# v as two adjacent keys per partition: a chunked attention in front of two feed-forward layers, on one Trainium2 core

## The chip, the cores and the metric

The program runs on 1 core of one Trainium2 chip. The metric is the device time of one execution in microseconds (us). The engines are named as the profile names them: PE (TensorE), PEld (its weight loads), DVE (VectorE), ACT (ScalarE), POOL (GpSimd) and SP (SyncE, which here only issues DMAs).

## What is computed

```python
q_c = q.reshape(B, H, nc, 64, D)              # B = H = 8, 576 tokens = 9 chunks of 64, D = 64; k_c, v_c alike
scores = (1 / np.sqrt(D)) * np.matmul(q_c, k_c.transpose(0, 1, 2, 4, 3))
scores = scores - np.max(scores, axis=-1, keepdims=True)
attn = np.exp(scores)
attn = attn / (np.sum(attn, axis=-1, keepdims=True) + 1e-09)
out = np.matmul(attn, v_c)
x = out.transpose(0, 2, 1, 3).reshape(4608, 512)
# logits = x @ w_gate; each of 8 experts takes 576 tokens, the largest logits first
# expert e: x = relu(x @ w1[e]) @ w2[e]
# last layer: max(x @ m1, x @ m2, x @ m3) @ m_out
```

## The kernel before, in words

The attention works on 9 units of 512 tokens (8 chunks of 64), each unit in 4 groups of 128 tokens with all 8 heads, 36 groups in all. The loop at L245 runs over the groups, and in iteration i it does one step of each of several groups: the scores of group i (`scores`, L124), the transposes and evacuations of a quarter of the q and k of the next unit (`trans`, `evac`, L105 and L117), the transposes of the weights of group i-1 (`att_t`, L164) and their product with v (`pv`, L175), and the scaling, storing and transposing of the result of group i-2 (`scale`, `x_t`, L185 and L192). The order of the calls is the order on each engine's queue. Once in four iterations a unit's logits are computed in two steps: `logit1` (L206, a product with w_gate in four column tiles) and `logit2` (L223, transposes and a sum on DVE), both through the PSUM bank pL.

v lies in three rotating buffers VB (L89). A buffer's partition is 64·s + key for head 2·hp + s, and its free part is [chunk, hp, s', d] with zeros where s' differs from s. So `pv` multiplies a stationary 128x64 tile (the transposed weights of two heads of one chunk) with 128 columns, 8 times in a group, in two column tiles of PE. A load of v (`load_v`, L65) writes 64 partitions; its contiguous pieces are one key of one head, 256 bytes. The zeros are written once at the start, half of them by two instructions for each buffer (L91, L92).

The loads of a unit's v are issued one unit ahead and those of q and k two units ahead, on SP's queue (half of v's on POOL's). At the top of each iteration SP issues a small DMA of the last maximum (`tick`, L249). It waits for that maximum, so that the loads behind it on SP's queue keep pace with the groups.

PSUM has 8 banks: pT has two buffers, pS takes two banks, and pA, pX, pY and pL have one each.

After the attention a router assigns the tokens in rounds, one for each expert (`Router.round`, L502). When the first round has named its expert, three 512 KB pieces ("chunks") of that expert's weights are issued on SP (L962 to L964), then POOL gathers the expert's 576 tokens in five indirect DMAs (`gather`, L793), and a second `tick` (L973) holds SP until the last of the five has landed. Each chunk is split into a high part by ACT (`split_hi`, L756) and a low part by DVE (`split_lo`, L765). A planner places these: `issue` (L744) gives a chunk a due time, 10 slots after its issue (16 for every eighth), `pump` (L946) moves the clock on by one slot per half of a product of 12 matmuls and calls `bulk` (L778), which splits a chunk whose time has come; `have` (L1017) splits at once what the next product needs. From the second expert on, PE has work throughout.

Of the kernel before, what the change touches and what calls it, by code (L numbers as in the profile page):

```python
# [7 lines left out]
F32 = mybir.dt.float32  # L8
# [20 lines left out]
def attention(ctx, tc, q, k, v, wg_in, xd, L, ident, consts, early, tick, mark):  # L29

    nc = tc.nc
    C = ctx.enter_context(tc.tile_pool(name="ac", bufs=1))
    P = ctx.enter_context(tc.tile_pool(name="aw", bufs=2))
    PS = ctx.enter_context(tc.tile_pool(name="aps", bufs=2, space=PSUM))
    QK, QT, KBT, PT, PSS, MX, A, R, PA, AT, PX, X, PY, XT, LS = ({} for _ in range(15))

    ORDER = [0, 1, 2, 3, None, 4, 5, 6, 7]

    def chunk(u, j):

        b = ORDER[u]
        return (b, b % 2 + j) if b is not None else (j, 0 if j % 2 else 8)
# [21 lines left out]

    def load_v(u, part):  # L65

        t = VB[u % 3]
        if ORDER[u] is not None:
            b, c = chunk(u, 0)
            for s in range(2):  # L70
                (nc.gpsimd if u and s else nc.sync).dma_start(
                    t[s * 64:(s + 1) * 64, :, part, s, :],
                    bass.AP(tensor=v.tensor, offset=v.offset + (b * H + 2 * part + s) * S * D + c * 64 * D,
                            ap=[[D, 64], [64 * D, 8], [1, D]]))
            return
        for j in (2 * part, 2 * part + 1):
            b, c = chunk(u, j)
            for s in range(2):
                (nc.gpsimd if u and s else nc.sync).dma_start(
                    t[s * 64:(s + 1) * 64, j, :, s, :],  # L80
                    bass.AP(tensor=v.tensor, offset=v.offset + b * H * S * D + s * S * D + c * 64 * D,
                            ap=[[D, 64], [2 * S * D, 4], [1, D]]))
# [6 lines left out]
    VB = [C.tile([128, 8, 4, 2, 64], F32, name="vb%d" % i) for i in range(3)]  # L89
    for t, eng in ((VB[0], nc.vector), (VB[1], nc.gpsimd), (VB[2], nc.gpsimd)):  # L90
        eng.memset(t[0:64, :, :, 1, :], 0.0)  # L91
        eng.memset(t[64:128, :, :, 0, :], 0.0)  # L92
    nc.scalar.dma_start(wg[:, :, :8], wg_in.rearrange("(a p) e -> p a e", p=128))
    consts()
    warm = PS.tile([128, 4, 128], F32, name="pA", bufs=1)
# [9 lines left out]
    def trans(nm, u, n, bank="pT"):  # L105

        mark(nm + "T")
        if n == 0:
            QT[nm, u] = P.tile([128, 4, 8, 64], F32, name=nm + "T")
        pt = PS.tile([128, 2, 2, 128], F32, name=bank, bufs=2 if bank == "pT" else 1)  # L110
        PT[nm, u, n] = pt
        for a in range(2):
            for w in range(2):
                h = 4 * (n // 2) + 2 * a + n % 2
                nc.tensor.transpose(pt[:, a, w, :], QK[nm, u][:, h, w * 128:w * 128 + 128], ident)  # L115

    def evac(nm, u, n, r, eng):  # L117
        mark(nm + "E")
        s, h0 = n % 2, 2 * (n // 2)
        src = PT[nm, u, n][r * 64:r * 64 + 64].rearrange("p a w t -> p a t w")  # L120
        dst = QT[nm, u][s * 64:s * 64 + 64, h0:h0 + 2].rearrange("p a j (i w r) -> p a (j i) w r", w=2, r=2)[:, :, :, :, r]
        (nc.vector.tensor_copy if eng else nc.scalar.copy)(dst, src)

    def scores(g):  # L124
        mark("scores")
        u, h = divmod(g, 4)
        PSS[g] = PS.tile([128, 2, 512], F32, name="pS", bufs=1)[:, :, :256].rearrange("p s (a i) -> p a s i", a=4)
        for hp in range(4):
            for c in range(2):
                for s in range(2):  # L130
                    o, to = slice(s * 64, s * 64 + 64), slice(c * 64, c * 64 + 64)
                    nc.tensor.matmul(PSS[g][to, hp, s], QT["q", u][o, hp, 2 * h + c], QT["k", u][o, hp, 2 * h + c],  # L132
                                     start=True, stop=True, tile_position=(s * 64, c * 64))
# [11 lines left out]

    def expo(g):
        mark("exp")
        e = P.tile([128, 8, 64], F32, name="A")
        nc.scalar.activation(e, A[g], AF.Exp, scale=0.125)
        A[g] = e  # L150

    def sums(g, st):
        mark("sums")
        if st == 0:
            R[g] = P.tile([128, 8], F32, name="sm")
            nc.vector.tensor_reduce(R[g], A[g], op=OP.add, axis=AX.X)
        elif st == 1:
            nc.vector.tensor_scalar(R[g], R[g], 1e-9, None, op0=OP.add)
        else:
            r = P.tile([128, 8], F32, name="rc")  # L160
            nc.vector.reciprocal(r, R[g])
            R[g] = r

    def att_t(g):  # L164
        mark("attT")
        PA[g] = PS.tile([128, 4, 128], F32, name="pA", bufs=1)
        for hp in range(4):
            nc.tensor.transpose(PA[g][:, hp, :], A[g][:, 2 * hp:2 * hp + 2, :], ident)  # L168

    def att_c(g):  # L170
        mark("attTc")
# [3 lines left out]
    def pv(g):  # L175
        mark("pv")
        u, h = divmod(g, 4)
        PX[g] = PS.tile([128, 4, 128], F32, name="pX", bufs=1)
        for hp in range(4):
            for c in range(2):  # L180
                nc.tensor.matmul(PX[g][c * 64:(c + 1) * 64, hp, :], AT[g][:, hp, c * 64:c * 64 + 64],  # L181
                                 VB[u % 3][:, 2 * h + c, hp].rearrange("p s i -> p (s i)"),
                                 start=True, stop=True)

    def scale(g):  # L185
        mark("scale")
        X[g] = P.tile([128, 8, 64], F32, name="x", bufs=3)
        nc.vector.tensor_tensor(X[g], PX[g].rearrange("p a (s i) -> p (a s) i", s=2),
                                R[g][:, :, None].to_broadcast([128, 8, 64]), op=OP.mult)
# [16 lines left out]
    def logit1(j, w0=0, w1=4):  # L206
        mark("logit1")
        t = slice(w0 * 128, w1 * 128)
        pl = PS.tile([128, 512], F32, name="pL", bufs=1)
        for dc in range(4):  # L210
            nc.tensor.matmul(pl[32 * dc:32 * dc + 32, t], wg[:, dc, :], XT[j][:, dc, t],
                             start=True, stop=True, tile_position=(0, 32 * dc))
        LS[j] = P.tile([128, 512], F32, name="ls")
        nc.scalar.copy(LS[j][:, t], pl[:, t])

    def logit(j, w):
        mark("logit")
        pl = PS.tile([128, 4, 128], F32, name="pT")
        for dc in range(4):
            nc.tensor.matmul(pl[:, 0, :E], XT[j][:, dc, w * 128:(w + 1) * 128], wg[:, dc, :E], start=dc == 0, stop=dc == 3)  # L220
        nc.vector.tensor_copy(L[:, columns(j)[w], :], pl[:, 0, :E])

    def logit2(j, w0=0, w1=4):  # L223
        mark("logit2")
        pl = PS.tile([128, 4, 4, 32], F32, name="pL", bufs=1)
        for w in range(w0, w1):
            nc.tensor.transpose(pl[:, w].rearrange("p a e -> p (a e)"), LS[j][:, w * 128:(w + 1) * 128], ident)
        to = columns(j)
        step = to[1] - to[0]
        nc.vector.tensor_reduce(L[:, to[w0]:to[w1 - 1] + 1:step, :],  # L230
                                pl[:, w0:w1, :, :8].rearrange("p w a e -> p w e a"), op=OP.add, axis=AX.X)

    banks = iter(("pT", "pT", "pX", "pY", "pL", "pA", "pT", "pT"))
    for n in (0, 2):
        for nm in "kq":
            for i in (n, n + 1):
# [4 lines left out]
    def on(j):  # L241
        return 0 <= j < G

    LOADS = [[("k", 0), ("q", 0)], [("k", 4)], [("q", 4)], []]
    for i in range(G):  # L245
        u, n = i // 4 + 1, i % 4
# [11 lines left out]
            scale(i - 2)  # L258
        if on(i):
            smax(i)  # L260
        if on(i - 1):
            att_t(i - 1)
            att_c(i - 1)
            if i < G - 1:
                sums(i - 1, 0)
# [17 lines left out]
        if on(i - 1):  # L283
            pv(i - 1)
            sums(i - 1, 1)
            sums(i - 1, 2)
        if i >= 7 and (i - 4) % 4 == 3 and i < G - 1:
            logit2((i - 4) // 4)
        if i >= 6 and (i - 3) % 4 == 3 and i < G:
            logit1((i - 3) // 4)  # L290
        if on(i - 2):
            x_c(i - 2)

# [16 lines left out]
    early(2)  # L310
    for st in (1, 2, 3):
        early(0, st)
    logit(8, 2)
    logit2(8, 0, 2)
    logit(8, 3)


class Clock:
# [381 lines left out]
def kernel(ctx, tc, q, k, v, w_gate, w1, w2, m1, m2, m3, m_out, out, mark=lambda n: None):  # L700
# [259 lines left out]
    rt.begin(PS)  # L960
    first = rt.round(0, PS, expert)
    while next(first) is not None:  # L962
        if state["issued"] < 3:
            issue()  # L964
    xg = gather(0)
    rt.warm(PS, 24)
# [3 lines left out]
            pass  # L970
        rt.warm(PS, (6, 5)[i])

    nc.sync.dma_start(tick[:, 4:5], xg[4][0:1, 0:1])  # L973

    split()
    XO, WA, WB, Y = {}, [], [], []
# [318 lines left out]
```

## Time and profile before

| | us |
|---|---|
| median of 3 runs (lowest to highest) | 1206.3 (1203.97 to 1208.42) |
| the profiled execution's own time | 1207.02 |
| its span, from the first to the last instruction | 1205.2 |
| PE busy | 1172.5 (97%) |
| DVE busy | 830.5 (69%) |
| ACT busy | 412.7 (34%) |
| POOL busy | 317.9 (26%) |

The shares are means over stages that differ: the attention takes about the first 165 us, the first round of the router the next 25, and the experts and the last layer the rest. How the rows are read: a row of the timeline has its start, its length, engine, line, operation, tiles, and in brackets how long the engine was idle before it and what ended that. A tile's name stands for all its buffers. An fp32 matmul shows as two instructions, a transpose as one.

### The profile page before, as it was taken

To read this page: it belongs to the slowest core of one execution; us is meant where nothing else is said; L and a number is where in the kernel's file an instruction comes from. 1 tells how busy PE (TensorE), PEld (TensorE's weight loads), DVE (VectorE), ACT (ScalarE), POOL (GpSimd) and SP (SyncE) were. 2 spreads that over 40 slices of the span, in tenths; PEclk is the share of its full clock that TensorE was granted. 3 is DMA by queue.
4 is the path that set the end of the run, shared out by engine and by line. 5 is a ranking of instruction groups with operands and counts; after the bars stand their busy time and mean duration, and the time that the engine had idled before them with its cause. 6 is when DMAs were issued, how large, how long until landed. Compare 5 with 4: busy or idle time off the path is not lost.

```text
span 1205.2 us, 23575 instructions
## 1 busy us (share of the span) xinstructions
PE 1172.5 (97%) x9508; PEld 1097.6 (91%) x9508; DVE 830.5 (69%) x1660; ACT 412.7 (34%) x674; POOL 317.9 (26%) x507
## 2 busy tenths in 40 slices
PE   7999978999999999999999999999999999999998
PEld 6788856989999999989999998998998998998996
DVE  6888976788898888888843565565565565664661
ACT  5888823232333333325423113113113113113111
POOL 8433201010337463766770002002002002002002
PEclk9999989999999999999999999999999999999999
DMA  9999516264566565559834773773773763773651
GB/s 264 256 271 269 162 45 184 66 233 150 177 193 209 184 215 183 186 192 283 281 144 162 274 259 123 276 260 119 280 259 118 281 259 115 285 258 114 235 189 53
DMA packets 138828, 242.99 MB, mean 202 GB/s; under 512 B 30048, under 2 KB 101216, under 8 KB 131808
## 3 DMA queue, kind: packets, MB, share of 16 engines
q1 hardware_dynamic: 118608, 180.90, 45.9%
q0 software_dynamic: 14976, 51.13, 12.7%
q10 hardware_dynamic: 5136, 9.46, 2.1%
q8 instruction: 75, 1.23, 0.4%
q14 instruction: 33, 0.27, 0.1%
HBM read 195.05 MB, written 46.40 MB: 200 GB/s over the span
## 4 chain that ended last, share of the span: by engine, by line
PE 53%; issue 35%; DMA 4%; DVE 3%; POOL 2%; ACT 1%; POOLq 1%; SPq 1%; ACTq 0%; DVEq 0%
PE acc L1105 17%; PE acc L1050 16%; DMA vb<-in_v_dram 3%; PE pX L181 2%; PE py L1143 2%; POOL out_dram L1227 2%; PE pT L115 2%; PE po L1219 2%; PE px L1143 2%; PE pz L1143 2%; PE pS L132 1%; PE pA L168 1%; PE pxt L821 1%; PE pY L199 1%; PE rp L553 1%
## 5 line engine op out<-in xcount | busy, mean ns | idle before, releaser
L1050 PE MATMUL acc<-xhi,chunk 128*128 128x288 f32 (+2 forms) x1024 | 207.4, 302 | 2.7 <-DVE hlo L1083 2.3
L1105 PE MATMUL acc<-hhi,chunk 128*128 128x288 f32 x1024 | 209.9, 299 | 0.0
L1227 POOL DMA_INDIRECT out_dram<-ot,ia x36 | 36.3, 1008 | 519.4 <-ACT ot L1225 518.8
L1050 PEld LDWEIGHTS acc<-xhi,chunk 128*128 128x128 f32 x1024 | 161.9, 189 | 3.8 <-DVE hlo L1083 2.7
L1105 PEld LDWEIGHTS acc<-hhi,chunk 128*128 128x128 f32 x1024 | 163.0, 188 | 0.3
L1105 PE MATMUL acc<-hlo,chunk 128*128 128x288 f32 x512 | 150.9, 295 | 0.0
L1219 PE MATMUL po<-chunk,h 128*128 128x512 f32 x648 | 149.3, 390 | 0.0
L1219 PEld LDWEIGHTS po<-chunk,h 128*128 128x128 f32 x648 | 121.5, 188 | 24.8
L1050 PE MATMUL acc<-xlo,chunk 128*128 128x288 f32 (+2 forms) x512 | 143.9, 296 | 0.0
L1143 PE MATMUL px<-xb,wa 128*128 128x384 f32 x648 | 130.0, 335 | 0.7 <-ACT ys L1112 0.7
L1143 PE MATMUL py<-xt,wb 128*128 128x384 f32 x648 | 129.9, 335 | 0.0
L1143 PEld LDWEIGHTS px<-xb,wa 128*128 128x128 f32 x648 | 113.9, 188 | 1.4 <-ACT ys L1112 1.0
L1143 PEld LDWEIGHTS py<-xt,wb 128*128 128x128 f32 x648 | 114.0, 188 | 0.5
L1164 ACT CAST h<-best 128x384 fp32r<-128x384 f32 x72 | 37.0, 513 | 198.1 <-DVE best L1162 121.3
L1105 PEld LDWEIGHTS acc<-hlo,chunk 128*128 128x128 f32 x512 | 96.2, 188 | 0.0
L1050 PEld LDWEIGHTS acc<-xlo,chunk 128*128 128x128 f32 x512 | 94.1, 189 | 0.0
L768 DVE TENSOR_TENSOR chunk<-raw,chunk 128x1024 fp32r<-128x1024 f32 x67 | 84.8, 1271 | 6.5 <-ACT chunk L761 5.7
L1074 ACT ACTIVATE hhi<-acc 128x576 fp32r<-128x576 f32 (+1 forms) x66 | 41.8, 637 | 137.2 <-PE acc L1050 135.3
L798 POOL DMA_INDIRECT xg<-xd,idx x40 | 43.3, 1082 | 169.2 <-DVE ohe L688 89.7
L1179 ACT COPY tmp<-px 128x384 f32<-128x384 f32 x54 | 25.8, 478 | 146.3 <-PE px L1143 146.3
L761 ACT CAST chunk<-raw 128x1024 fp32r<-128x1024 f32 x67 | 69.7, 1047 | 7.8 <-ACT ys L1112 6.4
L1083 DVE SCALAR_TENSOR_TENSOR hlo<-acc,hhi 128x576 fp32r<-128x576 f32 (+1 forms) x66 | 48.2, 735 | 30.9 <-ACT hhi L1074 30.5
(222 smaller groups left out, 2058.5 us busy)
## 6 DMA issues: line engine op xcount, KB each, us to landing
wb<-wdb SPq DMA_DIRECT2D x54, 1024.0 KB
wa<-wda SPq DMA_DIRECT2D x54, 768.0 KB
raw<-in_moe_w_dram SPq DMA_DIRECT2D x64, 512.0 KB
xd<-x POOLq DMA_DIRECT2D x36, 256.0 KB, 4.8
yd<-ys ACTq DMA_DIRECT2D x32, 288.0 KB
wdb<-pair POOLq DMA_DIRECT2D x18, 512.0 KB, 4.7
yraw<-yd SPq DMA_DIRECT2D x12, 768.0 KB
ink<-in_k_dram SPq DMA_DIRECT2D x16, 512.0 KB
```

The lines of the kernel that those rows point to most:

```text
L761: nc.scalar.copy(hi, raw)
L768: nc.vector.tensor_tensor(lo, raw, hi.bitcast(F32), op=OP.subtract)
L798: nc.gpsimd.indirect_dma_start(out=g, out_offset=None, in_=xd[:, :], in_offset=bass.IndirectOffsetOnAxis(ap=rt.idx[r][:, t:t + 1], axis=0))
L1050: nc.tensor.matmul(acc[:, hf, :tk.stop - tk.start], w[a][:, dc, o:o + 128], x[:, dc, tk], start=n == 0, stop=n == 11)
L1074: nc.scalar.activation(hv, src, AF.Relu)
L1083: nc.vector.scalar_tensor_tensor(lv, src, 0.0, hv.bitcast(F32), op0=OP.max, op1=OP.subtract)
L1105: nc.tensor.matmul(acc[:, hf, :288], w[a][:, f, :], x[:, f, tk], start=n == 0, stop=n == 23)
L1143: nc.tensor.matmul(dst, w[:, dc, o, a], XO[x][:, c, dc], start=start and n == 0, stop=stop and n == 5, skip_group_check=True)
L1164: nc.scalar.copy(hpart(g, i, j)[0], M)
L1179: nc.scalar.copy(U[g, 1], XB[g])
L1219: nc.tensor.matmul(PO[t], h[:, x, t % 6 * 128:t % 6 * 128 + 128], w[a][:, f % 2], start=f == 0 and n == 0, stop=f == 5 and n == 2)
L1227: st = nc.gpsimd.indirect_dma_start(out=out, out_offset=bass.IndirectOffsetOnAxis(ap=ia[:, t:t + 1], axis=0), in_=ot, in_offset=None)
```

## The change

v is laid out anew: a partition holds two adjacent keys of a head, so that a contiguous piece is 512 bytes, and a load writes 32 partitions. A buffer's partition is 64·i + 32·s + key pair, its free part [chunk, x, s', r, d], and the head is 4·i + 2·s + x. Each buffer is cleared by one instruction. The keys of k are left in the order in which the transposes give them (contiguous evacuations), and `scores` reads them in the order (r, i, w), two neighbouring columns lying 512 bytes apart. The exponential writes its result in the order that the new product wants, and the sums are taken over two axes. `pv` becomes 16 products of 64x64 tiles in place of 8 of 128x64, in two accumulating steps, and its result takes two PSUM banks. In exchange pL is given up: the logits use the two buffers of pT, and stand at another place of the loop, between the scores and the transposes of the weights, `logit1` one iteration later than before. Ahead of the first gather SP issues two chunks of weights and not three, and the `tick` behind the gather waits for its third piece and not for the fifth.

```diff
     def load_v(u, part):
-        t = VB[u % 3]
...
+        t, (x, i) = VB[u % 3], divmod(part, 2)
+        for s in range(2):
+            rows, head = slice(64 * i + 32 * s, 64 * i + 32 * s + 32), 4 * i + 2 * s + x
+            for e in range(1 if ORDER[u] is not None else 2):
+                b, c = chunk(u, e)
+                dst, n, step = (t[rows, :, x, s], 8, 64 * D) if ORDER[u] is not None else (t[rows, e::2, x, s], 4, 2 * H * S * D)
                 (nc.gpsimd if u and s else nc.sync).dma_start(
...
+                    dst.rearrange("p j r d -> p j (r d)"),
+                    bass.AP(tensor=v.tensor, offset=v.offset + (b * H + head) * S * D + c * 64 * D,
+                            ap=[[2 * D, 32], [step, n], [1, 2 * D]]))
...
-        eng.memset(t[0:64, :, :, 1, :], 0.0)
-        eng.memset(t[64:128, :, :, 0, :], 0.0)
+        eng.memset(t, 0.0)
...
     def evac(nm, u, n, r, eng):
...
+        if nm == "k":
+            src = PT[nm, u, n][r * 64:r * 64 + 64]
+            dst = QT[nm, u][s * 64:s * 64 + 64, h0:h0 + 2].rearrange("p a j (x t) -> p a (j x t)", x=2).rearrange(
+                "p a (r w t) -> p a r w t", r=2, w=2)[:, :, r]
...
     def scores(g):
...
+        keys = QT["k", u].rearrange("p a j x -> p a (j x)").rearrange("p a (r w j i) -> p a j r i w", r=2, w=2, j=8)
...
-                    nc.tensor.matmul(PSS[g][to, hp, s], QT["q", u][o, hp, 2 * h + c], QT["k", u][o, hp, 2 * h + c],
+                    nc.tensor.matmul(PSS[g][to, hp, s], QT["q", u][o, hp, 2 * h + c], keys[o, hp, 2 * h + c],
                                      start=True, stop=True, tile_position=(s * 64, c * 64))
...
     def expo(g):
-        e = P.tile([128, 8, 64], F32, name="A")
-        nc.scalar.activation(e, A[g], AF.Exp, scale=0.125)
+        e = P.tile([128, 4, 4, 32], F32, name="A")
+        nc.scalar.activation(e.rearrange("t n a p -> t a n p"), A[g].rearrange("t (a s) (r p) -> t a (s r) p", s=2, r=2),
+                             AF.Exp, scale=0.125)
...
-            nc.vector.tensor_reduce(R[g], A[g], op=OP.add, axis=AX.X)
+            nc.vector.tensor_reduce(R[g].rearrange("t (a s) -> t a s", s=2), A[g].rearrange("t (s r) a p -> t a s r p", r=2),
+                                    op=OP.add, axis=AX.XY)
...
     def pv(g):
...
-        PX[g] = PS.tile([128, 4, 128], F32, name="pX", bufs=1)
-        for hp in range(4):
-            for c in range(2):
-                nc.tensor.matmul(PX[g][c * 64:(c + 1) * 64, hp, :], AT[g][:, hp, c * 64:c * 64 + 64],
-                                 VB[u % 3][:, 2 * h + c, hp].rearrange("p s i -> p (s i)"),
-                                 start=True, stop=True)
+        PX[g] = PS.tile([128, 2, 512], F32, name="pX", bufs=1)
+        for x in range(2):
+            for r in range(2):
+                for c in range(2):
+                    for i in range(2):
+                        o = slice(i * 64, i * 64 + 64)
+                        nc.tensor.matmul(PX[g][c * 64:(c + 1) * 64, i, :256].rearrange("p (s x d) -> p x s d", s=2, x=2)[:, x],
+                                         AT[g][o, 2 * x + r, c * 64:c * 64 + 64], VB[u % 3][o, 2 * h + c, x, :, r],
+                                         start=r == 0, stop=r == 1, tile_position=(i * 64, c * 64))
...
     def logit1(j, w0=0, w1=4):
-        pl = PS.tile([128, 512], F32, name="pL", bufs=1)
+        pl = PS.tile([128, 512], F32, name="pT")
...
     def logit2(j, w0=0, w1=4):
-        pl = PS.tile([128, 4, 4, 32], F32, name="pL", bufs=1)
+        pl = PS.tile([128, 4, 4, 32], F32, name="pT")
...
         if on(i):
             smax(i)
+        if i >= 7 and i % 4 == 3:
+            logit1(i // 4 - 1)
+        if i >= 8 and i % 4 == 0:
+            logit2(i // 4 - 2)
         if on(i - 1):
             att_t(i - 1)
...
-        if i >= 7 and (i - 4) % 4 == 3 and i < G - 1:
-            logit2((i - 4) // 4)
-        if i >= 6 and (i - 3) % 4 == 3 and i < G:
-            logit1((i - 3) // 4)
...
-        if state["issued"] < 3:
+        if state["issued"] < 2:
             issue()
...
-    nc.sync.dma_start(tick[:, 4:5], xg[4][0:1, 0:1])
+    nc.sync.dma_start(tick[:, 4:5], xg[2][0:1, 0:1])
```

Left out: the scaling reads the two banks of the product, the first unit's transposes go to pX's two halves and not to pL, and the last token's logits use the bank pY.

## Rows read from the trace of the kernel before

**Rows 1.** The page: DMA busy share in 40 slices of 30 us.
```profile
DMA  9999516264566565559834773773773763773651
```

**Rows 2.** Stretches (us): length, busy PE, PEld, DVE, ACT, POOL, PE clock, DMA share, GB/s.
```profile
20.00:30.00 10.00, 8.84 (x134) 7.63 (x132) 6.58 (x12) 5.69 (x10) 7.66 (x24) 0.83 1.14 279
...
40.00:60.00 20.00, 18.22 (x275) 15.32 (x274) 15.44 (x31) 15.30 (x28) 10.13 (x18) 0.91 1.10 252
...
64.87:80.73 15.86, 15.86 (x270) 13.23 (x272) 14.30 (x30) 14.32 (x26) 6.58 (x11) 1.00 1.10 271
```

**Rows 3.** Timeline of PE, 16.9 to 58 us: the waits for loads.
```profile
19.66 0.44 PE L181 MATMUL pX<-vb,AT 128*64 128x128 f32 x4 [1.78 <-DMA vb<-in_v_dram]
...
22.47 1.09 PE L115 MATMUL pT<-ident,inq 128*128 128x128 f32 x4 [1.16 <-DMA inq<-in_q_dram]
...
55.74 0.44 PE L181 MATMUL pX<-vb,AT 128*64 128x128 f32 x4 [1.78 <-DMA vb<-in_v_dram]
```

**Rows 4.** The chain of waits: start, length, what.
```profile
41.70 13.90 DMA vb<-in_v_dram
```

**Rows 5.** Timeline of PE, 101 to 106 us: one iteration without logits.
```profile
101.75 0.69 PE L132 MATMUL pS<-kT,qT 64*64 64x64 f32 x32
102.38 0.66 PE L168 MATMUL pA<-ident,A 128*128 128x128 f32 x4
...
104.28 1.09 PE L181 MATMUL pX<-vb,AT 128*64 128x128 f32 x16
105.30 0.69 PE L132 MATMUL pS<-kT,qT 64*64 64x64 f32 x32
```

**Rows 6.** Timeline of DVE, 102 to 107 us: one iteration without logits.
```profile
102.34 0.69 DVE L188 TENSOR_TENSOR x<-pX,rc 128x512 f32<-128x512 f32 x1
102.95 0.68 DVE L138 TENSOR_REDUCE mx<-pS 128x8 f32<-128x512 f32 x1
...
104.91 0.69 DVE L122 COPY kT<-pT 64x512 f32<-64x512 f32 x1
...
106.14 0.69 DVE L188 TENSOR_TENSOR x<-pX,rc 128x512 f32<-128x512 f32 x1
```

**Rows 7.** Groups by form, 0 to 175 us: busy us, mean ns, idle before.
```profile
L230 DVE TENSOR_REDUCE L<-pL 128x32 f32<-128x128 f32 x8 | 2.3, 290 | 0.2
```

**Rows 8.** DMA totals of three stretches: 4 to 11, 13 to 17, 206 to 207.4 us.
```profile
DMA packets 2885, 2.39 MB, mean 341 GB/s; under 512 B 568, under 2 KB 2885, under 8 KB 2885
...
DMA packets 3041, 0.78 MB, mean 195 GB/s; under 512 B 3029, under 2 KB 3040, under 8 KB 3040
...
DMA packets 846, 0.43 MB, mean 308 GB/s; under 512 B 5, under 2 KB 846, under 8 KB 846
```

**Rows 9.** Waits of PEld, 64.5 to 144 us: total, times, longest.
```profile
PEld pS L132 <- issue: 6.5, 17, 0.8
...
PEld pX L181 <- issue: 1.7, 10, 0.2
```

**Rows 10.** Timeline by engine, 184 to 262 us: first gather, splitting of weights, one wait.
```profile
188.48 1.06 POOL L798 DMA_INDIRECT xg<-xd,idx  x1 [21.96 <-DVE idx L682]
...
193.56 0.66 PE L821 MATMUL pxt<-ident,xg 128*128 128x128 f32 x4 [1.58 <-DMA xg<-xd,idx]
...
202.98 1.22 DVE L768 TENSOR_TENSOR chunk<-raw,chunk 128x1024 fp32r<-128x1024 f32 x1
...
211.32 0.32 PEld L1050 LDWEIGHTS acc<-xhi,chunk 128*128 128x128 f32 x2
...
211.75 1.22 DVE L768 TENSOR_TENSOR chunk<-raw,chunk 128x1024 fp32r<-128x1024 f32 x1
...
214.92 0.24 PE L566 MATMUL rp<-cs,lev 128*128 128x8 f16 x4 [0.61 <-DVE cs L558]
```

**Rows 11.** The tile xg: time from issue to landing of its 40 DMAs.
```profile
DMA to landing us min/median/max: 3.4/4.2/7.3
```

**Rows 12.** Weight loads by form, 185 to 189 us (72 bytes between columns).
```profile
L665 PEld LDWEIGHTS <-aoh 128*32 128x32 bf16 x36 | 0.6, 155 | 0.7 <-DVE aoh L642 0.7
```

More of the change, by code (lines that the diff above doesn't have):

```diff
@@ L65, in load_v @@
     def load_v(u, part):
-        t = VB[u % 3]
-        if ORDER[u] is not None:
-            b, c = chunk(u, 0)
-            for s in range(2):
-                (nc.gpsimd if u and s else nc.sync).dma_start(
[L72 to L82, printed above, removed]
+        t, (x, i) = VB[u % 3], divmod(part, 2)
[4 more added lines that the diff above has]
+                dst, n, step = (t[rows, :, x, s], 8, 64 * D) if ORDER[u] is not None else (t[rows, e::2, x, s], 4, 2 * H * S * D)
+                (nc.gpsimd if u and s else nc.sync).dma_start(
+                    dst.rearrange("p j r d -> p j (r d)"),
+                    bass.AP(tensor=v.tensor, offset=v.offset + (b * H + head) * S * D + c * 64 * D,
+                            ap=[[2 * D, 32], [step, n], [1, 2 * D]]))
     for h in (0, 4):
@@ L88, in attention @@
     nc.vector.memset(wg, 0.0)
-    VB = [C.tile([128, 8, 4, 2, 64], F32, name="vb%d" % i) for i in range(3)]
+    VB = [C.tile([128, 8, 2, 2, 2, 64], F32, name="vb%d" % i) for i in range(3)]
     for t, eng in ((VB[0], nc.vector), (VB[1], nc.gpsimd), (VB[2], nc.gpsimd)):
-        eng.memset(t[0:64, :, :, 1, :], 0.0)
-        eng.memset(t[64:128, :, :, 0, :], 0.0)
+        eng.memset(t, 0.0)
     nc.scalar.dma_start(wg[:, :, :8], wg_in.rearrange("(a p) e -> p a e", p=128))
@@ L109, in trans @@
             QT[nm, u] = P.tile([128, 4, 8, 64], F32, name=nm + "T")
-        pt = PS.tile([128, 2, 2, 128], F32, name=bank, bufs=2 if bank == "pT" else 1)
+        if isinstance(bank, str):
+            pt = PS.tile([128, 2, 2, 128], F32, name=bank, bufs=2 if bank == "pT" else 1)
+        else:
+            pt = bank.rearrange("p (a w t) -> p a w t", a=2, w=2)
         PT[nm, u, n] = pt
@@ L120, in evac @@
         src = PT[nm, u, n][r * 64:r * 64 + 64].rearrange("p a w t -> p a t w")
-        dst = QT[nm, u][s * 64:s * 64 + 64, h0:h0 + 2].rearrange("p a j (i w r) -> p a (j i) w r", w=2, r=2)[:, :, :, :, r]
+        if nm == "k":
+            src = PT[nm, u, n][r * 64:r * 64 + 64]
+            dst = QT[nm, u][s * 64:s * 64 + 64, h0:h0 + 2].rearrange("p a j (x t) -> p a (j x t)", x=2).rearrange(
+                "p a (r w t) -> p a r w t", r=2, w=2)[:, :, r]
+        else:
+            dst = QT[nm, u][s * 64:s * 64 + 64, h0:h0 + 2].rearrange("p a j (i w r) -> p a (j i) w r", w=2, r=2)[:, :, :, :, r]
         (nc.vector.tensor_copy if eng else nc.scalar.copy)(dst, src)
@@ L166, in att_t @@
         PA[g] = PS.tile([128, 4, 128], F32, name="pA", bufs=1)
-        for hp in range(4):
-            nc.tensor.transpose(PA[g][:, hp, :], A[g][:, 2 * hp:2 * hp + 2, :], ident)
+        for n in range(4):
+            nc.tensor.transpose(PA[g][:, n, :], A[g].rearrange("t n a p -> t n (a p)")[:, n], ident)
     def att_c(g):
@@ L177, in pv @@
         u, h = divmod(g, 4)
-        PX[g] = PS.tile([128, 4, 128], F32, name="pX", bufs=1)
-        for hp in range(4):
-            for c in range(2):
-                nc.tensor.matmul(PX[g][c * 64:(c + 1) * 64, hp, :], AT[g][:, hp, c * 64:c * 64 + 64],
-                                 VB[u % 3][:, 2 * h + c, hp].rearrange("p s i -> p (s i)"),
-                                 start=True, stop=True)
+        PX[g] = PS.tile([128, 2, 512], F32, name="pX", bufs=1)
[7 more added lines that the diff above has]
+                                         start=r == 0, stop=r == 1, tile_position=(i * 64, c * 64))
     def scale(g):
@@ L187, in scale @@
         X[g] = P.tile([128, 8, 64], F32, name="x", bufs=3)
-        nc.vector.tensor_tensor(X[g], PX[g].rearrange("p a (s i) -> p (a s) i", s=2),
-                                R[g][:, :, None].to_broadcast([128, 8, 64]), op=OP.mult)
+        nc.vector.tensor_tensor(X[g].rearrange("p (i h) d -> p i h d", i=2),
+                                PX[g][:, :, :256].rearrange("p i (h d) -> p i h d", d=64),
+                                R[g].rearrange("p (i h) -> p i h", i=2)[:, :, :, None].to_broadcast([128, 2, 4, 64]), op=OP.mult)
         nc.gpsimd.dma_start(xd[tokens(g) * 128:(tokens(g) + 1) * 128, :], X[g].rearrange("p h d -> p (h d)"))
@@ L214, in logit1, with logit @@
         nc.scalar.copy(LS[j][:, t], pl[:, t])
-    def logit(j, w):
+    def logit(j, w, bank):
         mark("logit")
-        pl = PS.tile([128, 4, 128], F32, name="pT")
+        pl = PS.tile([128, 4, 128], F32, name=bank, bufs=2 if bank == "pT" else 1)
         for dc in range(4):
@@ L231, in logit2 @@
                                 pl[:, w0:w1, :, :8].rearrange("p w a e -> p w e a"), op=OP.add, axis=AX.X)
-    banks = iter(("pT", "pT", "pX", "pY", "pL", "pA", "pT", "pT"))
+    px = PS.tile([128, 2, 512], F32, name="pX", bufs=1)
+    banks = iter(("pT", "pT", "pY", px[:, 0], px[:, 1], "pA", "pT", "pT"))
     for n in (0, 2):
@@ L312, in attention @@
         early(0, st)
-    logit(8, 2)
+    logit(8, 2, "pT")
     logit2(8, 0, 2)
-    logit(8, 3)
+    logit(8, 3, "pY")
 class Clock:
```

## The prediction

> **What bounds the kernel now.** I read the page first. Its line of DMA shares [rows 1] shows the DMA engines busy in the first four slices of 30 us and little used right after them. So the part that the change rewrites, the attention, is the part in which transfers can matter. The table of stretches [rows 2] splits it. From 20 to 60 us PE falls short of the time, and the granted clock is below one: 0.83 in 20 to 30 us, 0.91 in 40 to 60 us. From 64.87 us on PE is busy throughout at the full clock, and a unit of four groups takes 15.86 us. The timeline of PE names what it waited for earlier [rows 3]: 1.78 us for v at 19.66 us, 1.16 us for q at 22.47 us and 1.78 us for v at 55.74 us, 4.72 us in all. The clock fell behind such gaps. Below the full clock a stretch loses the missing share, here 10 x 0.17 = 1.7 us and 20 x 0.09 = 1.8 us, so that loads that come late cost about 4.7 + 3.5 = 8.2 us. The chain of waits has the load behind the last of them [rows 4]: issued at 41.70 us, it took 13.90 us to land. It stood in a full queue.
>
> After 60 us the bound is PE, though only just. An iteration without logits takes PE 105.30 - 101.75 = 3.55 us [rows 5]. The same iteration takes DVE 106.14 - 102.34 = 3.80 us [rows 6]. DVE falls 0.25 us behind in each such iteration and catches up in those with logits, where PE has more to do. Per unit DVE needs 4 x 3.80 + 0.2 for the logits' sum (0.29 us long [rows 7], partly overlapped) = 15.4 us, against PE's 15.86. A faster PE can thus gain 0.45 us a unit, and then DVE is the bound.
>
> **The load of v.** A unit's v is 1.05 MB. While v alone is transferred, in pieces of 256 bytes, the rate is 195 GB/s; q and k, in pieces of 1 KB, run at 341, and a weight matrix in pieces of 512 bytes at 308 [rows 8]. A unit's v costs 1.05/195 = 5.4 us of transfer now, and 1.05/308 = 3.4 us at the rate of 512-byte pieces: 2.0 us less a unit. That is the upper end. The rates differ in a second thing, however: v writes 64 partitions and the weights 128, and the new load writes 32. If the few partitions set the rate, nothing is gained; that is the lower end. Nothing here excludes a rate under 195 either, but the pieces of the new load are larger in any case. I take 1.35 us a unit, two thirds, because for nearly all units other transfers run beside v and fill what one load leaves free. [...]
>
> Three units of v have to land before the last wait (the one at 55.74 us is in group 9, whose unit is the third). 3 x 1.35 = 4.0 us: that wait would end at 51.7 us. PE can be there by then: with the two waits at 20 us shortened and DVE's 3.80 us an iteration it gets there near 51 us. So the transfers give 4.0 us up to there. With a wait of under a microsecond in place of 1.78, I count on most of the 1.8 us of slow clock in 40 to 60 us to come back, 1.5 us; the slow clock in 20 to 30 us stays in my sum. SP's queue issues as many loads of v as before, POOL's too, each with half as many pieces.
>
> **PE in an iteration.** `pv` streams 8 x 128 columns through two column tiles now, and 16 x 128 through four tiles then: the same time, if four work at once. The scores show that they do: 16 products of 64 columns start within 102.38 - 101.75 = 0.63 us, against 1.02 us for `pv` [rows 5]; twice the columns of the scores would be at most 1.26 us, the upper end. I take 1.02. PEld stands idle 0.17 us ahead of `pv` (1.7 us in 10 times), and as a rule ahead of the scores as well [rows 9], at every change between whole array, 128x64 and 64x64. With `pv` in 64x64 tiles the change ahead of the scores goes. With the logits moved beside the scores, the four iterations of a unit have 9 such changes where they had 14 (`logit2` works on the whole array, like the transposes behind it). 5 x 0.17 = 0.85 us, to 15.0 us a unit; at the lower end nothing goes. But DVE needs 15.4. And `logit1` now takes a buffer of pT, which is free only after ACT's last evacuation of q of the iteration before; PE would wait there, with the transposes queued behind. Between DVE's 15.4 and the 15.86 of now I take 15.6: 0.26 us for each of some 5 units after 62 us, 1.4 us. In the last four groups, where PE waits for ACT and nothing runs beside it, four changes less are 4 x 0.17 = 0.7 us.
>
> **Costed at nothing.** The exponential, the sums over two axes, the evacuation of k and the scaling move as many elements as before; a copy that reads PSUM at 512-byte distances takes DVE 0.69 us against 0.68 for a reduction of a contiguous block as wide [rows 6], so order counts for little there. The cover is thin: what DVE's sums took more, would count in full, 36 times. Clearing a buffer goes over as many columns in one instruction as before in two, under the first loads of q and k.
>
> **The gather.** Its first piece is issued at 188.48 us and used at 193.56 us [rows 10], 5.1 us later, where such pieces land in 4.2 us (median), 3.4 at the least [rows 11]. Without the third chunk ahead of it I take 4.2: 0.9 us gained, 0 to 1.7 as bounds. Against it: the third chunk, split by 202.98 us now, is issued with the fourth then, and so becomes due ten slots after that. It takes the place of the fourth, whose low part DVE makes at 211.75 us for 1.22 us. Its first product begins at 211.32 us and would wait until 213.0: 1.6 us. The wait of 0.61 us at 214.92 us, behind DVE's next split [rows 10], would then be covered. So 1.0 us is lost, and the two make 0; from -1.7 to +1.6 as bounds. SP is let go earlier, by the third piece, and the chunks behind it land long before they are due.
>
> **The sum.** 4.0 + 1.5 + 1.4 + 0.7 + 0 = 7.6 us off 1207.0, the profiled execution's own time, is 1199.4; it lies 0.7 us above the median of 1206.3, from which the same sum gives 1198.7. About 0.5% (6 us) is what a measurement of this kernel can tell from no change.
>
> **The rivals.**
> - Every late load goes. At 308 GB/s or better, with PE no longer idle at 20 us, the clock holds too: 8.2 us less the 1.5 us by which DVE slows the first iterations, plus 1.4, 0.7 and the 0.9 of the gather = 9.7: 1196.6, and 1195 if DVE is not in the way. For it: the row of 512-byte pieces. Against it: all of it has to come together.
> - v lands no sooner, since 32 partitions set the rate. Then 1.4 + 0.7 is left, 2.1 us: 1204.2. For it: 195 GB/s is measured with few partitions. Against it: other transfers share the time.
> - The changes of tiling cost as much as before, because the gap belongs to each new batch of weights and not to the tile. Then 4.0 + 1.5 is left: 1200.8, or 1202 with the new wait of `logit1` uncovered.
> - Slower: the scores' moving operand. Two columns of it now lie 512 bytes apart, in each of 16 products of a group, 36 times. PE has 0.25 us in an iteration without logits until it is later than DVE, plus the 0.17 saved. If a column took three times as long, 2 x 0.46 = 0.92 us more in an iteration (0.63 less the change), 0.5 us would be beyond the cover, 36 x 0.5 = 18 us, less the 5.5 of the loads: 12.5 us, 1219. It decides from 0.42 + 5.5/36 = 0.57 us more in an iteration, a column at 2.2 times its time; at twice the time a small gain would be left. [...]
>
> **How the numbers follow.** The forecast of 7.6 us has a chance of 0.50; its own range is 1194.5 to 1203, from the bounds of the load and the gather, and three quarters of it lie over 6 us: 0.37 faster, 0.13 the same. Every late load goes: 0.17, faster. v no sooner: 0.14, the same. Tiling as before: 0.05, the same. Slower: 0.14. So 0.54 faster, 0.32 the same, 0.14 slower. 1192 to 1207 takes in all cases but the last and the outer edges of the first two, 2 in 10 left out.
>
> **What would show it.** Right: no wait for v or q over 1 us before 60 us, and a clock of one in 40 to 60 us; transfers of v alone above 250 GB/s; no idle time of PEld between `pv` and the scores, and a unit near 15.6 us with DVE busy throughout; the first gathered piece used 4.2 us after its issue, and a new wait of PE for a chunk's low part near the expert's fifth product. Wrong: scores over 0.8 us, sums over 0.75 us, or v at 195 GB/s again.

## The result, and the profile after

The changed kernel takes 1213.6 us (median of 6 runs, 1211.7 to 1216.9), the kernel before 1205.6 us beside it: a ratio of 1.0064, 95% interval 1.0043 to 1.0084. It is slower by 8 us, where 7.6 us less had been forecast; the time lies outside the range. The profiled execution has a span of 1210.5 us (before: 1205.2).

The pieces of the loads became larger, as the change asked. On the page, in the packets' line, those under 512 bytes fell to a third (9568; 30048 before), and the DMA share, which answers to [rows 1], is as high as it was:

```profile
DMA  9999714373636565658854663763763773773651
...
DMA packets 128592, 243.05 MB, mean 201 GB/s; under 512 B 9568, under 2 KB 90976, under 8 KB 121568
...
q8 instruction: 79, 1.29, 0.5%
```

The stretches, with the columns of [rows 2]: the last row is one unit of four groups in the steady part.

```profile
20.00:30.00 10.00, 7.96 (x176) 6.81 (x166) 8.52 (x18) 7.92 (x14) 7.20 (x23) 1.00 1.11 298
40.00:60.00 20.00, 15.86 (x327) 13.60 (x326) 14.38 (x30) 14.18 (x25) 9.43 (x17) 1.00 1.00 191
60.00:80.00 20.00, 17.67 (x301) 15.45 (x304) 12.73 (x26) 12.66 (x23) 5.55 (x10) 0.83 0.94 213
124.13:140.30 16.17, 15.78 (x334) 13.67 (x333) 14.24 (x30) 14.23 (x26) 4.64 (x8) 1.00 0.93 257
```

The rate in 20 to 30 us rose from 279 to 298 GB/s, and the clock is 1.00 there and, as forecast, in 40 to 60 us. But PE is busy for only 15.86 us of 40 to 60 us, where it was 18.22; then the clock falls to 0.83 in 60 to 80 us, and the unit has 16.17 us where it had 15.86.

What PE waited for before 66 us (us in total, times, longest) has no load in it any more; the waits of [rows 3] are gone. Another kind stands in their place:

```profile
PE pS L134 <- issue: 7.6, 3, 4.5
PE pA L90 <- POOL ident L360: 1.8, 1, 1.8
PE pX L111 <- DVE qT L123: 1.8, 1, 1.8
PE pX L188 <- issue: 1.5, 2, 1.0
```

The third row stands in no term of the prediction: two sets of the first unit's transposes now share the tile pX, and the second waits until DVE has evacuated the first. The first group's maxima come at 15.06 us, where the kernel before has 13.01; how much of that is left after the first units, no run shows.

"issue" means that PE waited for nothing that the profile shows. The timeline of PE has these idle times one by one, in the middle of runs of equal products, where neither the tiles nor the shapes change:

```profile
23.28 0.97 PE L188 MATMUL pX<-vb,AT 64*64 64x128 f32 x25 [0.51 <-issue]
...
31.11 0.49 PE L134 MATMUL pS<-kT,qT 64*64 64x64 f32 x12 [2.25 <-issue]
...
38.52 0.74 PE L188 MATMUL pX<-vb,AT 64*64 64x128 f32 x14 [0.95 <-issue]
...
44.21 0.35 PE L134 MATMUL pS<-kT,qT 64*64 64x64 f32 x4 [0.88 <-issue]
...
61.94 0.48 PE L134 MATMUL pS<-kT,qT 64*64 64x64 f32 x5 [4.50 <-issue]
...
102.43 0.23 PE L134 MATMUL pS<-kT,qT 64*64 64x64 f32 x1 [1.80 <-issue]
```

Together they are 10.9 us. The kernel before has one, of 0.30 us at 110.81 us. **Their places are the clue.** Counted in matmuls as the profile records them (an fp32 product is two), they come after 217, 342, 466, 590, 841 and 1589 of them: the distances are 125, 124, 124, 2 x 125.5 and 6 x 124.7. 124.7 matmuls with a weight load each are 249 instructions. The DMA totals list a queue of instructions, q8, in packets of 16 KB: 79 of them, where the kernel before has

```profile
q8 instruction: 75, 1.23, 0.4%
```

The counts say whose instructions they are. All six runs with 16 products in `pv` have 79 packets for PE's 20168 matmuls and weight loads, all seven with 8 have 75 for 19016: 255 and 254 for each packet. The 249 between two idle places are close to that; I take them for what one packet brings and call them a block. In stretches of 0.2 us its packets can be placed; this is the one of 58.6 to 58.8 us:

```profile
q8 instruction: 1, 0.02, 50.8%
```

| block of 124.7 begins | next packet of q8 | next block begins | idle (issue) |
|---|---|---|---|
| after: 23.28 | 28.2 | 31.11 | 2.25 |
| after: 31.11 | 35.8 | 38.52 | 0.95 |
| after: 38.52 | 41.4 | 44.21 | 0.88 |
| after: 44.21 | 45.8 | 52.88 | 0 |
| after: 52.88 | 58.6 | 61.94 | 4.50 |
| before: 25.93 | 29.6 | 33.57 | 0 |
| before: 40.90 | 44.8 | 48.13 | 0 |
| before: 48.13 | 54.0 | 56.98 | 0 |

(Where no idle time marks it, a block's begin is read off the timeline by counting matmuls from the idle times, to some 0.2 us; for the kernel before, from the one at 110.81 us.) A packet moves 1.6 to 5.9 us after the block ahead of it has begun, and each idle time ends 2.7 to 3.3 us after a packet. In the kernel before, the next block begins 3.0 to 4.0 us after the packet: just in time.

The two other parts of the change. In the steady part the border of a unit has a new wait, here in the timelines of PE and of ACT:

```profile
138.84 0.57 PE L134 MATMUL pS<-kT,qT 64*64 64x64 f32 x18
139.80 0.50 PE L134 MATMUL pS<-kT,qT 64*64 64x64 f32 x14 [0.39 <-ACT qT L123]
140.23 0.66 PE L235 MATMUL pT<-ident,ls 128*128 128x128 f32 x4
```

```profile
139.14 0.60 ACT L123 COPY qT<-pT 64x512 f32<-64x512 f32 x1
```

The next unit's scores need ACT's last evacuation of q. At the gather, the first piece is issued at 198.09 us and used at 201.54 us, and a chunk's low part is waited for later (timelines of POOL and PE):

```profile
198.09 1.05 POOL L807 DMA_INDIRECT xg<-xd,idx  x1 [21.88 <-DVE idx L691]
```

```profile
201.54 0.66 PE L830 MATMUL pxt<-ident,xg 128*128 128x128 f32 x4
...
221.73 0.40 PE L1059 MATMUL acc<-xhi,chunk 128*128 128x288 f32 x1 [1.28 <-DVE chunk L777]
```

### The profile page after: what moved, and what is told of

It reads as the page before. It is cut to its first block, busy times and chain, and to the rows that moved or that the text cites. A ratio compares the mean times of both kernels' runs of the same rounds, so it can differ in the third digit from the quotient of the medians.

```text
span 1210.5 us, 24703 instructions
## 1 busy us (share of the span) xinstructions
PE 1172.2 (97%) x10084; PEld 1101.7 (91%) x10084; DVE 826.9 (68%) x1659; ACT 412.0 (34%) x674; POOL 308.8 (26%) x505
## 2 busy tenths in 40 slices
DMA packets 128592, 243.05 MB, mean 201 GB/s; under 512 B 9568, under 2 KB 90976, under 8 KB 121568
## 4 chain that ended last, share of the span: by engine, by line
PE 51%; issue 36%; DVE 4%; ACT 4%; POOL 3%; DMA 1%; POOLq 1%; ACTq 0%; DVEq 0%
PE acc L1114 17%; PE acc L1059 16%; PE py L1152 2%; POOL out_dram L1236 2%; PE po L1228 2%; PE pX L188 2%; PE px L1152 2%; PE pz L1152 2%; PE pT L111 1%; PE pS L134 1%; PE pxt L830 1%; ACT qT L123 1%; PE pA L172 1%; PE rp L562 1%; ACT AT L177 1%
```

## The experiments

**Theory A**: PE's instructions come too late, since their blocks wait in DMA queues that the loads keep full (DMA share 1.00 to 1.11 in 20 to 60 us), and the 8 more products in each group, 16 more recorded matmuls with 16 weight loads (80 pairs in place of 64), use a block up sooner. **Theory B**: the logits' new place and their shared bank make the loss.

**As many instructions in the kernel before.**

```diff
-                nc.tensor.matmul(PX[g][c * 64:(c + 1) * 64, hp, :], AT[g][:, hp, c * 64:c * 64 + 64],
-                                 VB[u % 3][:, 2 * h + c, hp].rearrange("p s i -> p (s i)"),
-                                 start=True, stop=True)
+                for s in range(2):
+                    nc.tensor.matmul(PX[g][c * 64:(c + 1) * 64, hp, s * 64:s * 64 + 64], AT[g][:, hp, c * 64:c * 64 + 64],
+                                     VB[u % 3][:, 2 * h + c, hp, s], start=True, stop=True)
```

> The kernel before, with each product of pv (128 columns) cut into two of 64: as many matmuls and weight loads in a group as the changed kernel has, and nothing else of the change (v's old layout and loads, logits in their old place, old gather). Theory A, PE's instructions come too late: PE's stream is fetched in blocks over DMA queues that are full until 60 us or later; a block holds the instructions of about 124.7 recorded matmuls, the kernel before uses one up in 7.2 to 8.8 us while the queues are full, and just gets the next in time; with 25% more instructions in a group it does not. Then PE shows idle times put down to issue at distances of 124.7 matmuls, 5 to 10 us in all before 110 us, and the kernel takes 1209 to 1216 us. Theory B, the loss lies in the new order of the logits and in the bank that they share with the transposes, and the idle times put down to issue belong to the new loads of v: no such idle time over 1 us here, and 1204 to 1208 us.

Measured: 1.0054 (1.0038 to 1.0069), 1213.2 us. The idle times appear, 251 matmuls apart, in the middle of the scores (timeline of PE):

```profile
46.89 0.34 PE L132 MATMUL pS<-kT,qT 64*64 64x64 f32 x8 [1.94 <-issue]
...
61.39 0.27 PE L132 MATMUL pS<-kT,qT 64*64 64x64 f32 x1 [2.62 <-issue]
```

With 0.30 us at 38.92 us they are 4.9 us, just under the 5 to 10 that A expected; the unit also grew to 16.18 us, which makes another 1.9 us in six units. So more products of the same columns do it alone, with the old layout of v and the old place of the logits, and B's 1204 to 1208 us is excluded.

**As few instructions in the changed kernel.**

```diff
-        for x in range(2):
-            for r in range(2):
...
-                        nc.tensor.matmul(PX[g][c * 64:(c + 1) * 64, i, :256].rearrange("p (s x d) -> p x s d", s=2, x=2)[:, x],
-                                         AT[g][o, 2 * x + r, c * 64:c * 64 + 64], VB[u % 3][o, 2 * h + c, x, :, r],
+                    nc.tensor.matmul(PX[g][c * 64:(c + 1) * 64, i, :256].rearrange("p (s x d) -> p x s d", s=2, x=2),
+                                     AT[g][o, r, c * 64:c * 64 + 64], VB[u % 3][o, 2 * h + c, :, :, r],
...
```

> The changed kernel with 8 products of 256 columns in pv in place of 16 of 128: the same columns streamed, the same 64x64 tiles, the same loads of v, but as many instructions in a group as the kernel before. Left out: the weights of half of the heads (each product uses the weights of the even head for the odd one as well). Theory A (instructions come too late): idle times put down to issue shrink from about 10.9 us before 110 us to 2 at most, the clock in 60 to 80 us is 1.0 again, and the time is 1202 to 1207 us. Theory B (logits and their bank; the idle times belong to v's loads): the idle times stay, 1212 to 1215 us.

Measured: 0.9962 (0.9949 to 0.9975), 1201.4 us: 12 us under the changed kernel, and a little better than A's 1202 to 1207. No idle time put down to issue is left before 190 us, and the stretches are whole again:

```profile
40.00:60.00 20.00, 19.30 (x336) 14.96 (x329) 17.27 (x36) 17.15 (x31) 9.94 (x18) 1.00 1.08 280
60.00:80.00 20.00, 19.19 (x331) 15.30 (x330) 17.19 (x37) 17.13 (x30) 7.14 (x14) 1.00 1.00 271
```

The columns streamed, the tiles and the loads are those of the changed kernel. The 12 us (9 to 15 by the two intervals) are the price of 8 more products a group, 16 recorded matmuls and 16 weight loads. The unit stays at 16.17 us, so that one has another cause.

**Lighter queues, the same instructions.**

```diff
-        if tr:
+        if tr and u < 2:
             load_v(u, n)
```

> The changed kernel with v loaded for the first three units alone; left out are v's loads of all later units, which use what their buffers hold. PE's instructions are the same. Theory A (a block of PE's instructions comes late because its packet waits behind the loads in full DMA queues): from the third unit's loads on the queues are lighter, and the idle times put down to issue after 40 us shrink from 7.2 us (0.9, 4.5 and 1.8) to 2 at most; 1204 to 1209 us. Rival (PE cannot take more than so many instructions in a time, or pays at each block, whatever the queues hold): the idle times after 40 us stay at 5 to 8 us, 1211 to 1215 us.

Measured: 1.0006 (0.9989 to 1.0023), 1206.4 us, and the timeline of PE has two idle times left:

```profile
30.87 0.55 PE L134 MATMUL pS<-kT,qT 64*64 64x64 f32 x12 [2.25 <-issue]
...
58.12 0.35 PE L134 MATMUL pS<-kT,qT 64*64 64x64 f32 x3 [1.76 <-issue]
```

The first, ahead of the missing loads, is as long as it was; after 40 us 7.2 us shrank to 1.76. A fixed price of a block, or a limit of PE itself, would have stayed. The packet of the last one moved at 54.8 us, 3.3 us ahead of its end, as in the table.

**The logits back in their old place**, with the loads and `pv` of the change and pT's banks.

```diff
-        if i >= 7 and i % 4 == 3:
-            logit1(i // 4 - 1)
-        if i >= 8 and i % 4 == 0:
-            logit2(i // 4 - 2)
...
+        if i >= 7 and (i - 4) % 4 == 3 and i < G - 1:
+            logit2((i - 4) // 4)
+        if i >= 6 and (i - 3) % 4 == 3 and i < G:
+            logit1((i - 3) // 4)
```

> The changed kernel with the logits' two steps back behind pv, where they stood before; they still use pT's banks. Theory A (instructions come too late): idle times put down to issue stay at 8 to 11 us before 110 us; the unit after 62 us goes from 16.2 us to 15.6 to 15.9, 0.3 to 0.6 us in each of some 6 units, so 2 to 4 us of the 8 are gained: 1209.5 to 1211.5 us. Theory B (the logits' new order makes most of the loss): 1207 us or less.

Measured: 1.0043 (1.0027 to 1.0059), 1212.4 us. B is out. The idle times put down to issue are 6.4 us, where 8 to 11 had been expected: with the same products they differ from run to run, 8.9 and 9.2 us in the two other runs with the whole of the change's `pv` and loads. But the unit went the wrong way, from 16.17 to 16.67 us (16.67 us between the logits' sums in the timeline of DVE), because the logits now wait for a bank of pT, here among PE's waits of 23 to 111 us:

```profile
119.90 0.29 DVE L238 TENSOR_REDUCE L<-pT 128x32 f32<-128x128 f32 x1 [0.31 <-PE pT L235]
136.57 0.29 DVE L238 TENSOR_REDUCE L<-pT 128x32 f32<-128x128 f32 x1 [0.31 <-PE pT L235]
```

```profile
PE pT L235 <- DVE kT L123: 1.2, 4, 0.5
PE pT L219 <- DVE kT L123: 1.0, 2, 0.5
```

With the bank lost, the new place is the better one for the unit; in the time the two can't be told apart.

**Where the unit's 0.3 us come from.** One try takes a copy from ACT:

```diff
-        nc.scalar.copy(LS[j][:, t], pl[:, t])
+        nc.vector.tensor_copy(LS[j][:, t], pl[:, t])
```

> The changed kernel with the copy of the logits' products (ls) on DVE in place of ACT. Theory: the unit of 16.17 us comes from ACT's row of copies at the unit's border (ls ahead of AT, k's and q's evacuations, on which the next unit's scores wait); with 0.6 us less of it the unit goes to 15.7 to 15.9 us, 2 to 3 us in all: 1210 to 1212 us. Rival: PE itself takes 16.17 us with its 16 products more (the kernel before with pv split also has 16.18): the unit stays, 1212.5 to 1214.5 us.

Measured: 1.0086 (1.0066 to 1.0106), 1216.1 us, above both ranges; unit 16.23 us. The copy is not it; the rival named there, PE's additional products, was already out by the 16.17 us with 8 products in `pv`. The other try moves the logits alone, in the kernel before with the gather's part (two lines: `issued < 2`, `xg[2]`), with their own bank:

```diff
+        if i >= 7 and i % 4 == 3:
+            logit1(i // 4 - 1)
+        if i >= 8 and i % 4 == 0:
+            logit2(i // 4 - 2)
         if on(i - 1):
             att_t(i - 1)
...
-            logit2((i - 4) // 4)
...
-            logit1((i - 3) // 4)
```

> The kernel before with the gather's part and with the logits' two steps moved ahead of attT, as in the change, but in their own bank pL and with the old pv and v. Theory: the fewer changes of tiling on PE are worth 0.17 us each and nothing waits for pT: the unit goes from 15.86 to 15.4 to 15.7 us, and the time to 1198.5 to 1200.5 us. Rival: the copy ls ahead of AT on ACT holds up the unit's border as in the changed kernel: unit 15.9 to 16.2 us, 1201.5 to 1204 us.

Measured: 0.9995 (0.9978 to 1.0012), 1205.9 us; unit 16.28 us (115.19 to 131.47 us between the logits' sums). The unit went the rival's way, and the time lies above both ranges. The scores at the border wait as in the changed kernel (timeline of PE, then ACT):

```profile
128.42 1.09 PE L181 MATMUL pX<-vb,AT 128*64 128x128 f32 x16
129.44 0.56 PE L132 MATMUL pS<-kT,qT 64*64 64x64 f32 x18
130.34 0.45 PE L132 MATMUL pS<-kT,qT 64*64 64x64 f32 x14 [0.34 <-ACT qT L122]
130.72 0.66 PE L227 MATMUL pL<-ident,ls 128*128 128x128 f32 x4
```

```profile
129.68 0.60 ACT L122 COPY qT<-pT 64x512 f32<-64x512 f32 x1
```

In the kernel before, `logit2` stood ahead of these scores and was PE's work while ACT finished q; its timeline of PE shows no wait:

```profile
129.85 0.66 PE L227 MATMUL pL<-ident,ls 128*128 128x128 f32 x4
130.44 0.79 PE L132 MATMUL pS<-kT,qT 64*64 64x64 f32 x32
```

So the new place costs the unit 0.4 us, with or without a shared bank. That it does so by uncovering ACT's evacuation, with `logit2` on top, is read from these rows; no run took the evacuation away.

**The gather's part**, alone on the kernel before (twice), and undone in the changed kernel.

```diff
-        if state["issued"] < 3:
+        if state["issued"] < 2:
...
-    nc.sync.dma_start(tick[:, 4:5], xg[4][0:1, 0:1])
+    nc.sync.dma_start(tick[:, 4:5], xg[2][0:1, 0:1])
```

> The kernel before with the gather's part of the change alone: two weight loads ahead of the first gather in place of three, and SP let go by the third gathered piece. Theory A and B say the same of it. As the traces of the two kernels have it: the first gathered piece is used about 1.6 us sooner after its issue, and the wait for the third chunk's low part (1.2 us) gives most of it back: 1204.5 to 1206 us, no difference. Rival: this part costs by itself, because the third chunk, asked for later, is late by more than the gather gains: 1207 to 1209 us.

> The kernel before with the whole of the gather's part once more, beside its halves. It brought 4.8 us on the kernel before and 0.9 us on the changed kernel, each with about 2 us either way. If the part is worth one amount whatever stands ahead of it, that is near the 2.4 us that the profiled execution shows behind the attention's end: 1202.5 to 1204.5 us. Rival: 4.8 us again: 1201 to 1202 us.

> The changed kernel with the gather's part undone (three weight loads ahead of the first gather, SP let go by the fifth piece). If that part is worth the 4.8 us that it brought the kernel before, whatever the attention does: 1217 to 1220 us. Rival: in the profiled executions only 2.4 us of that stood behind the attention's end, the rest was a shorter attention by chance; then 1214.5 to 1216.5 us.

Measured: 0.9957 (0.9942 to 0.9973) and 0.9978 (0.9963 to 0.9993) on the kernel before, 1201.5 and 1203.2 us: a gain larger than the 1204.5 to 1206 us expected at first, the second within its 1202.5 to 1204.5. Undone in the changed kernel it is 1.0072 (1.0054 to 1.0091), 1212.7 us, against 1.0064: no difference that can be told, where 1217 to 1220 or 1214.5 to 1216.5 us had been expected. A gain of 3.5 us lies within the intervals of all three. Of its halves, the two lines one by one:

> The kernel before with two weight loads ahead of the first gather in place of three; SP is still let go by the fifth gathered piece. Theory: the missing load makes the first piece land sooner (1.5 us), and the new due time of the third chunk moves DVE's later work, which shortens later waits: nearly all of the part's gain is here, 1202.5 to 1204.5 us. Rival: with SP let go late the third chunk lands too late and its wait grows from 1.3 us to 3 or more: 1206 us or above.

> The kernel before with SP let go by the third gathered piece in place of the fifth, and three weight loads ahead as before; every engine has the same instructions in the same order. Theory: nothing waits for the loads behind it, so no difference: 1205 to 1207 us. Rival: loads that start sooner run beside the last two pieces of the gather and hold them up: 1207 to 1209 us.

Measured: 0.9974 (0.9960 to 0.9988) with two loads, 0.9995 (0.9980 to 1.0009) with SP let go earlier. The gain is the missing load's; the other line shows none, though its interval leaves room for 2 us. Where it lies: PE's waits of 184 to 560 us, first in the kernel before, then with the whole part (second run).

```profile
PE acc L1050 <- DVE hlo L1083: 2.3, 1, 2.3
PE rp L566 <- DVE cs L558: 2.2, 3, 0.8
PE pxt L821 <- DMA xg<-xd,idx: 1.6, 1, 1.6
```

```profile
PE acc L1050 <- DVE chunk L768: 1.3, 1, 1.3
...
PE acc L1050 <- DVE hlo L1083: 0.9, 1, 0.9
PE rp L566 <- DVE cs L558: 0.5, 1, 0.5
```

The first piece gives 1.6 us, the third chunk takes 1.3, and two waits behind DVE, after the first gather, become 1.4 and 1.7 us shorter: 3.4 us, against 2.6 (0.22%) to 5.2 (0.43%) measured.

In the changed kernel there is less to gain: with the part undone, PE waits 0.2 us for gathered pieces and 1.3 us behind `hlo`, where the kernel before has 1.6 and 2.3.

The kernel before with the gather's part alone beats both kernels: 1201.5 and 1203.2 us.

## Why the prediction was wrong

**The step that failed** is the sentence on `pv`: "the same time, if four work at once". It counted columns, found them equal, and left the 16 recorded matmuls and 16 weight loads that a group gets on top out of the sum and out of every rival. Their supply cost 12 us (1.0064 against 0.9962 for the same columns in half as many products). In the profiled execution that is 10.9 us of idle time put down to issue, and 20 x 0.17 = 3.4 us of slow clock in 60 to 80 us behind the longest of them; the two make more than 12, so some of it did not reach the end. Rows 9 held the word "issue", and I read it as changes of tiling only; the packets of the instruction queue were on the page and I passed over them.

**Loads of v and slow clock, 4.0 + 1.5 us:** mis-sized. I took 1.35 us a unit, two thirds of the way to the 308 GB/s of the weights. In 13 to 17 us, the stretch in which [rows 8] has 195 GB/s, the changed kernel has 215:

```profile
DMA packets 1679, 0.86 MB, mean 215 GB/s; under 512 B 100, under 2 KB 1679, under 8 KB 1679
```

The last microsecond of that already holds pieces of q and k; in 12 to 16 us, with v alone, it is 217 GB/s, and 201 to 211 in the five experiments with the new load. At 217 a unit's v takes 1.05/217 = 4.84 us where it took 5.38, so 0.5 us are saved and not 1.35, 1.6 us for three units. That is nearly my second rival, v no sooner, and the sign "transfers of v alone above 250 GB/s" failed. Whether the 32 partitions set the rate no run separates. That PE does not wait for v in the changed kernel is no sign of faster loads, for PE gets there later: with 8 products it waits again, for v of the second unit.

```profile
35.72 1.30 PE L187 MATMUL pX<-vb,AT 64*64 64x256 f32 x13 [1.99 <-DMA vb<-in_v_dram]
```

The maxima of group 12 come at 63.0 us there. In the five executions with the old attention (the kernel before and the four runs that change the gather alone) they come at 64.8 to 67.4 us, and with the old loads and the logits moved at 64.5. So 1.5 to 4.4 us were gained up to there, not 5.5. In the changed kernel they come at 73.6 us: what was gained was lost in the same 60 us. Of the clock, 0.91 in 40 to 60 us was one execution's: the other four with the old attention have 0.95 to 1.00, so that its return is not shown to be the loads' doing.

**Steady state, 1.4 us of gain:** wrong in sign. In an iteration without logits the change of tiling did go, and `pv` hands over after 0.92 us where [rows 5] has 1.02:

```profile
126.40 1.10 PE L188 MATMUL pX<-vb,AT 64*64 64x128 f32 x32
127.32 0.73 PE L134 MATMUL pS<-kT,qT 64*64 64x64 f32 x32
127.98 0.33 PE L172 MATMUL pA<-ident,A 128*128 128x128 f32 x1
```

But I counted changes of tiling over the unit and not what `logit2` had covered. The unit has 16.17 us and not 15.6: 0.31 us lost in each of some six units, 1.9 us. DVE was not the bound that I made it: it was busy for 14.24 of the 16.17 us. The tail's 0.7 us did not come either: from the maxima of group 32 to the last logits it takes 18.5 us before (147.3 to 165.8) and 19.0 with 8 products (143.8 to 162.8).

**The gather, 0:** the parts that I saw came as forecast (used after 3.45 us, where I had 4.2 and 3.4 as the bound; a chunk's wait of 1.28 us, where I had 1.6). I followed the effect for 30 us only; the waits behind DVE that it shortened later are 3.1 us. Some 3.4 us gained on the kernel before, where I had none; on the changed kernel 1.0 us (1.0072 against 1.0064), not clear of nothing.

**The slower rival**, scores whose moving operand has 512 bytes between columns, gave the right sign by the wrong mechanism. No run shows the columns of three times the length that its 18 us assume: scores start the next work 0.66 us later (127.32 to 127.98 us), 0.63 in [rows 5]. **Costed at nothing** was right: in 62 to 160 us the sums take 675 ns as before, the exponential 633 ns against 630, the scaling 692 against 689:

```profile
L195 DVE TENSOR_TENSOR x<-pX,rc 128x512 f32<-128x512 f32 x23 | 15.9, 692 | 3.4 <-PE pX L188 1.5
L159 DVE TENSOR_REDUCE sm<-A 128x8 f32<-128x512 f32 x23 | 15.5, 675 | 0.0
...
L151 ACT ACTIVATE A<-A 128x512 f32<-128x512 f32 x23 | 14.6, 633 | 3.0 <-DVE A L145 1.8 <-DVE sm L162 0.5
```

By the measured terms: +12.3 for the instructions, +1.9 and +0.5 for steady state and tail, and -3.4 (as on the kernel before) to -1.0 (as on the changed kernel) for the gather. To reach the 8 us, the loads and the start are left with -3.3 to -5.7. That is a remainder, with 3 us of uncertainty in its largest term; it agrees with the 1.5 to 4.4 us of group 12 only at its small end and is no check of them.

One reading of the prediction is off without weight on this: the wait at 55.74 us is in the product of group 8 (its unit is the third all the same).

What stays open: the profile names no engine for a packet of instructions; that these are PE's rests on the counts, on the 2.7 to 3.3 us, and on the three runs that moved the idle times. Why the kernel before with `pv` split has 4.9 us of them and the changed kernel 10.9 (6.4 to 9.2 in three runs like it) was not tried. That a fetch starts only when the block ahead has begun fits the table, and no run shows it directly.

## What to carry to other kernels

Count instructions as well as columns: with 25% more of them in a group and the DMA queues busy, PE stood idle for 10.9 us here, and the same work in half as many products was worth 12 us. Idle time put down to "issue" in the middle of equal instructions, at equal counts, is the sign to look for. A rate taken from a load of another shape is a hope: 308 GB/s into 128 partitions became 217 into 32. And before a short step is moved off a border, ask which other engine's work it covered there.

## What the runs showed of the hardware

- PE stood idle up to 4.50 us at distances of one or more times 124 to 125.5 recorded matmuls with their weight loads (some 249 instructions), each time until 2.7 to 3.3 us after a 16 KB packet of the instruction queue; with v's later loads left out, 7.2 us of it after 40 us became 1.76.
- That margin was already used up before: its next blocks began 3.0 to 4.0 us after their packets, and 25% more recorded matmuls in a group (64 to 80) were too many.
- v alone, in pieces of 512 bytes into 32 partitions, moved at 201 to 217 GB/s in six runs; in pieces of 256 bytes into 64 partitions at 191 to 196 in seven (13 to 16 us).
- The same attention code reached group 12 at 64.8 to 67.4 us in five executions: differences of 2 us between single profiles of this part say nothing.
